# One decode step of attention with a gated unit: a kernel in a scheduling framework rewritten with hand-written waits, pairs of heads, three slots

## The chip, the cores and the metric

The kernel runs on one core of a Trainium2 chip. The core has TensorE (PE: matmuls, with PEld for loading their weights), VectorE (DVE), ScalarE (ACT), GpSimd (POOL) and SyncE (SP). SP and ACT issue transfers (DMA) between the chip's main memory and the on-chip memory, which has 128 partitions; 16 DMA engines carry them. The metric is the time of one execution in microseconds on the device, as the median of several runs.

## The reference

One token `x` of 512 numbers is normalised and goes through attention with 32 heads against caches of 8192 keys and values of 128 numbers, all in 32-bit floats, and through a gated unit. The two results are multiplied and added to `x`.

```python
xn = layernorm(x)                                   # (1, 1, 512)
q = (xn @ wq).reshape(32 heads, 128)                # wq: 512 x 4096
scores = einsum("hd,hkd->hk", q, k_cache) * 128 ** -0.5
o = einsum("hk,hkd->hd", softmax(scores), v_cache)  # caches: 32 x 8192 x 128
s = o.reshape(4096) @ wo                            # wo: 4096 x 512
h = sigmoid(xn @ w_gate) * (xn @ w_up)              # 512 x 1376 each
g = silu(h @ w_down)                                # w_down: 1376 x 512
out = x + s * g
```

K and V of one head are 4 MB each, 268 MB in all heads; `wq` and `wo` are 8 MB each, the three gate matrices 2.8 MB each.

## The kernel before

The kernel is written in a framework that places the waits, with the order of instructions written out by hand (`manual_schedule`). Each load goes into one of six slots of 32 KB a partition (`slot`, line 59). A head's K is one load of 4 MB in which each partition takes 64 keys, one row of 32 KB; V likewise. K and the weights are issued on SP's queue, V on ACT's (`load_rows`, line 96). `order` (line 110) is the order of loads: the two halves of wq, then K and V of each head, then the gate matrices and wo, in rows of 8 KB, between and behind the last heads; `need` issues ahead by it.

At the start, x is normalised (lines 155 to 167) and q is computed as matmuls with one column of weights, four of them side by side in four column groups of TensorE (line 182). `spread` copies the q of four heads to all partitions (line 192).

For each head, VectorE multiplies K by q and sums over the 128 numbers, in four blocks of 16 keys a partition (lines 258 and 259). It takes the maximum of each partition (line 263); TensorE turns these into a row (line 265) of which VectorE takes the maximum (line 269), but only after the first block of the next head. TensorE sends the maximum to all partitions (line 271), ScalarE takes the exponential and its sum (line 275), and TensorE multiplies it with V: 16 matmuls of 4 weight columns and 512 moving columns in four column groups (line 284). ScalarE copies the result and TensorE folds the four diagonal blocks (lines 288 and 290). Every fourth head, VectorE normalises four heads and turns them into columns (`heads_out`).

The gate's matmuls stand in the last head and behind it (`glu_row`, `glu_hidden`, `glu_out`), then `project` multiplies with wo, four groups of 128 columns for each row, and the result is written.

Of the kernel before, what the change touches and what calls it, by code (L numbers as in the profile page):

```python
# [17 lines left out]
@with_exitstack
def kernel(
# [35 lines left out]
    ps_o = ctx.enter_context(tc.tile_pool(name="ps_o", bufs=1, space=bass.MemoryType.PSUM))
    ps_s = ctx.enter_context(tc.tile_pool(name="ps_s", bufs=1, space=bass.MemoryType.PSUM))


    def slot(name):
        return stream.tile([P, SLOT], F32, tag="stream", name=name)  # L60

    xv = x.rearrange("a b d -> (a b d)")
    x_col = const.tile([P, KT], F32, name="x_col")
    x_row = const.tile([P, GC], F32, name="x_row")
    wq_t, kv_t, wo_t, gl = {}, {}, {}, {}

    def load_wq(i):
        n = KT // 2
        t = slot(f"wq{i}").rearrange("p (k c) -> p k c", k=n)
        nc.sync.dma_start(t, wq.rearrange("(p k) c -> p k c", k=KT)[:, i * n:(i + 1) * n, :])  # L70
        for k in range(n):
            wq_t[i * n + k] = t[:, k, :]

    def load_gate(name, src):
        t = slot(name)
        t = t[:, :KT * F].rearrange("p (k f) -> p k f", f=F)
        nc.sync.dma_start(t, src.rearrange("(p k) f -> p k f", k=KT))
        for k in range(KT):
            gl[name, k] = t[:, k, :]
# [4 lines left out]
    FW = FP * GP
    assert FW + GP <= QT and FL % GP == 0

    def load_down():
        t = slot("wd")
        n = (FP + 1) * D
        gl["hid"] = t[:, n:n + (FP + 1) * GP].rearrange("p (c i) -> p c i", i=GP)  # L90
        t = t[:, :n].rearrange("p (c e) -> p c e", e=D)
        nc.sync.dma_start(t[:, :FP, :], w_down[:FP * P, :].rearrange("(p r) e -> p r e", r=FP))
        nc.sync.dma_start(t[:FL, FP, :], w_down[FP * P:, :])
        gl["wd"] = t

    def load_rows(which, src, h):
        t = slot(f"{which}{h}")
        q = nc.sync if which == "k" else nc.scalar
        q.dma_start(t, src[0, h].rearrange("(p j) d -> p (j d)", p=P))
        kv_t[which, h] = t  # L100

    def load_wo(g0, n):
        t = slot(f"wo{g0}").rearrange("p (g r e) -> p g r e", r=HT, e=D)
        for i in range(n):
            src = wo[(g0 + i) * P * HT:(g0 + i + 1) * P * HT, :].rearrange("(p r) e -> p r e", r=HT)
            for r0, r1 in ((0, HT),) if g0 + i < NW - 1 else ((0, HT - 1), (HT - 1, HT)):
                nc.sync.dma_start(t[:, i, r0:r1, :], src[:, r0:r1, :])
            wo_t[g0 + i] = t[:, i]

    order = [("wq", 0), ("wq", 1)]  # L110
    for h in range(H):
        order.append(("k", h))
        if h < H - 2:
            order.append(("v", h))
    order += [("v", H - 2), ("glu", 0), ("v", H - 1), ("glu", 1), ("glu", 2), ("wo", 0), ("wo", NW // 2)]

    def issue(which, i):
        if which == "wq":
            load_wq(i)
        elif which == "wo":  # L120
            load_wo(i, NW // 2)
        elif which == "glu":
            (lambda: load_gate("wg", w_gate), lambda: load_gate("wu", w_up), load_down)[i]()
# [3 lines left out]
    ahead = iter(order)
    loaded = set()

    def need(*item):  # L130
        while item not in loaded:
            nxt = next(ahead)
            issue(*nxt)
            loaded.add(nxt)

    nc.scalar.dma_start(x_col, xv.rearrange("(p k) -> p k", k=KT))
    need("v", 1)
    nc.vector.memset(x_row, 0.0)
    nc.scalar.dma_start(x_row[0:P:GP, :], xv.rearrange("(g c) -> g c", g=NG))


    ones = const.tile([P, P], F32, name="ones")
    nc.vector.memset(ones, 1.0)
    ident = const.tile([P, P], F32, name="ident")
    make_identity(nc, ident)
    eps_t = const.tile([P, 1], F32, name="eps_t")
    nc.vector.memset(eps_t, EPS)

    def total(col, name):
        t = ps_s.tile([P, 1], F32, tag="ps_s", name=name)  # L150
        nc.tensor.matmul(t, ones, col, start=True, stop=True)
        return t

    st = const.tile([P, 8], F32, name="st")
    nc.vector.reduce_sum(st[:, 0:1], x_col, axis=AX.X)  # L155
    p_sum = total(st[:, 0:1], "p_sum")
    nc.vector.tensor_scalar(st[:, 1:2], p_sum, 1.0 / D, None, op0=ALU.mult)
# [6 lines left out]
    nc.scalar.activation(st[:, 3:4], p_sq, AF.Sqrt, bias=eps_t, scale=1.0 / D)
# [2 lines left out]
    nc.vector.tensor_scalar(xn, xc, st[:, 4:5], None, op0=ALU.mult)
# [8 lines left out]
    q_row = const.tile([P, NQ // NG, QT], F32, name="q_row")
    pq = [big(f"pq{b}", 0.0) for b in range(NQ // NG)]
    for k in range(KT):
        for b in range(NQ // NG):
            for g in range(NG):  # L180
                c = (b * NG + g) * QT
                nc.tensor.matmul(pq[b][g * GP:g * GP + 1, :], xn[:, k:k + 1], wq_t[k][:, c:c + QT],  # L182
                                 start=(k == 0), stop=(k == KT - 1))
    for b in range(NQ // NG):
        nc.scalar.copy(q_row[:, b, :], pq[b])

    qb = {}

    def spread(t):
        b, g = divmod(t, NG)  # L190
        pb = big(f"pb{t}")
        nc.tensor.matmul(pb, ones[g * GP:g * GP + 1, :], q_row[g * GP:g * GP + 1, b, :],  # L192
                         start=True, stop=True)
        qb[t] = work.tile([P, QT], F32, tag="qb", name=f"qb{t}")
        nc.scalar.copy(qb[t], pb)  # L195


    g_row = const.tile([P, GC], F32, name="g_row")
    pgu = {}

    def glu_row(name):

        pgu[name] = big(f"p{name}", 0.0)
        for c0, f0, w, m in ((0, 0, FW, NG), (FW, P * FP, GP, FL // GP)):
            for k in range(KT):
                for g in range(m):
                    nc.tensor.matmul(pgu[name][g * GP:g * GP + 1, c0:c0 + w], xn[:, k:k + 1],
                                     gl[name, k][:, f0 + g * w:f0 + (g + 1) * w],
                                     start=(k == 0), stop=(k == KT - 1))

    def glu_hidden():

        sg, h = q_row[:, 0, :FW + GP], q_row[:, 1, :FW + GP]
        nc.scalar.activation(sg, pgu["wg"][:, :FW + GP], AF.Sigmoid)
        nc.vector.tensor_mul(h, sg, pgu["wu"][:, :FW + GP])
        for t in range(FP):
            nc.vector.transpose(gl["hid"][:, t, :], h[:, t:FW:FP])
        nc.vector.transpose(gl["hid"][:, FP, :], h[:, FW:])

    def glu_out():  # L220
        pd = big("pd", 0.0)
        for t in range(FP + 1):
# [151 lines left out]
```

## Time and profile before

| | us |
|---|---|
| median of 3 runs | 695.82 (695.55 to 696.3) |
| span of the profiled execution, first to last instruction | 693.6 |
| VectorE busy | 606.3 |
| TensorE busy, matmuls | 296.0 |
| VectorE waiting for K | 37.6 |
| VectorE's first product with K starts at | 51.90 |

The profile gives the profiled execution's span; its own time with what lies around the span is not listed, so the span stands against the median of the runs. Busy times are totals for an engine, so an engine can be busy for most of the span and still not be the one that the end waits for. In a row of a group, the numbers are the busy time, the mean of one instruction in nanoseconds, and the idle time of the engine ahead of these instructions with what ended it. In a row of a timeline they are the start and the length in microseconds, the engine, the line and the instruction, and in brackets the idle time before.

### The profile page before, as it was taken

Reading aid. Unit: us, or ns where it says so; the run is one execution under the profiler, and the core shown is the slowest. Engines: PE = TensorE matmul, PEld = TensorE weight load, DVE = VectorE, ACT = ScalarE, POOL = GpSimd, SP = SyncE. Lnnn points to the kernel's source line nnn. Section 1 sums busy time; section 2 is a strip of 40 time slices with the busy share of each in tenths; the row PEclk is TensorE's granted clock in tenths of the full one; section 3 lists DMA queues with packets and bytes.
Section 4 is the critical chain, followed back from the end, with each engine's and each line's share of the span. In section 5 each row is a group of like instructions: output and inputs, shape, how many; then the busy total and the mean of one; then the engine's idle time right before and its main releaser. Section 6 shows DMA issues by size and latency. Waiting matters only on the chain.

```text
span 693.6 us, 4841 instructions
## 1 busy us (share of the span) xinstructions
PE 296.0 (43%) x2012; PEld 89.6 (13%) x2012; DVE 606.3 (87%) x418; ACT 49.0 (7%) x144; POOL 0.7 (0%) x6
## 2 busy tenths in 40 slices
PE   0420454434343554445434444445443434444555
PEld 0000110111110111111111111111110110111224
DVE  1109999999999999999999999999989999999931
ACT  0010110001000010000000100001000100000010
POOL 0000000000000000000000000000000000000000
PEclk9855676766666666666766666666666666666789
DMA  9999999999999999999999999999999999999996
GB/s 384 433 423 431 443 425 422 438 437 425 426 439 433 424 429 438 430 426 427 438 433 425 434 431 435 424 433 435 429 427 431 438 426 427 430 437 427 424 387 252
DMA packets 11526, 293.98 MB, mean 424 GB/s; under 512 B 1416, under 2 KB 1424, under 8 KB 1776
## 3 DMA queue, kind: packets, MB, share of 16 engines
q1 hardware_dynamic: 6744, 159.45, 53.9%
q10 hardware_dynamic: 4760, 134.22, 45.0%
q8 instruction: 15, 0.25, 0.1%
q14 instruction: 7, 0.06, 0.0%
HBM read 293.67 MB, written 0.00 MB: 423 GB/s over the span
## 4 chain that ended last, share of the span: by engine, by line
DVE 74%; DMA 20%; another core or an unknown queue 5%; issue 1%; PE 0%; DVEq 0%; SPq 0%; ACT 0%
DVE sc L259 36%; DVE k L258 34%; DMA k<-in_A_k_cache_dram 11%; DMA wd<-in_B_w_down_dram 4%; DMA wo<-in_A_wo_dram 3%; DMA x_col<-in_A_x_dram 2%; DVE mx L263 1%; DVE mx L269 1%; DVE ot L300 1%; DVE on L297 0%; DVE o_all L301 0%; PE acc L306 0%; DVE po L238 0%; DVE pq L173 0%
## 5 line engine op out<-in xcount | busy, mean ns | idle before, releaser
L258 DVE TENSOR_TENSOR k<-k,qb 128x2048 f32<-128x2048 f32 x128 | 291.8, 2280 | 37.6 <-DMA k<-in_A_k_cache_dram 37.6
L259 DVE TENSOR_REDUCE sc<-k 128x16 f32<-128x2048 f32 x128 | 292.6, 2286 | 6.5
L284 PE MATMUL po<-v,pr 128*4 128x512 f32 x1024 | 182.9, 877 | 0.0
L265 PE MATMUL pt<-ident,mx 128*1 128x128 f32 x64 | 18.3, 386 | 192.8 <-DVE mx L263 192.8
L271 PE MATMUL pm<-mx,ones 1*128 1x1 f32 x64 | 18.6, 358 | 122.6 <-DVE mx L269 122.6
L284 PEld LDWEIGHTS po<-v,pr 128*4 128x4 f32 x1024 | 33.3, 110 | 118.6 <-issue 118.6
L290 PE MATMUL pn<-o,pick 128*1 128x128 f32 x256 | 33.1, 272 | 22.8 <-ACT o L288 22.8
L271 PEld LDWEIGHTS pm<-mx,ones 1*128 1x128 f32 x64 | 15.9, 307 | 145.6 <-DVE mx L269 145.6
L288 ACT COPY o<-po 128x512 f32<-128x512 f32 x32 | 18.8, 586 | 187.2 <-PE po L284 187.2
L265 PEld LDWEIGHTS pt<-ident,mx 128*1 128x1 f32 x64 | 2.8, 80 | 202.5 <-DVE mx L263 171.1
L272 ACT ACTIVATE mx<-pm 128x1 f32<-128x1 f32 x32 | 5.5, 171 | 331.8 <-PE pm L271 331.8
L290 PEld LDWEIGHTS pn<-o,pick 128*1 128x1 f32 x256 | 18.8, 83 | 58.6 <-ACT o L288 53.8
L182 PE MATMUL pq<-wq,xn 128*1 128x512 f32 x64 | 12.0, 917 | 11.4 <-DMA wq<-in_A_wq_dram 10.0
L280 PE MATMUL pn<-ones,rs 128*1 128x1 f32 x64 | 6.0, 164 | 24.7 <-ACT pr L275 24.7
L192 PE MATMUL pb<-q_row,ones 1*128 1x512 f32 x16 | 15.6, 1074 | 0.0
L275 ACT ACTIVATE pr<-sc,mx 128x64 f32<-128x64 f32 x32 | 11.1, 348 | 1.0
L155 DVE TENSOR_REDUCE st<-x_col 128x1 f32<-128x4 f32 x1 | 0.2, 157 | 12.0 <-DMA x_col<-in_A_x_dram 12.0
L195 ACT COPY qb<-pb 128x512 f32<-128x512 f32 x8 | 4.7, 586 | 67.4 <-PE pb L192 67.4
L269 DVE TENSOR_REDUCE mx<-pt 1x1 f32<-1x128 f32 x32 | 8.6, 269 | 0.5 <-PE pt L265 0.5
L295 DVE RECIPROCAL rl<-pn 128x1 f32<-128x1 f32 x8 | 1.2, 148 | 8.7 <-PE pn L290 8.7
L306 PE MATMUL acc<-wo,o_all 128*1 128x128 f32 x256 | 7.7, 272 | 2.5 <-issue 1.5
L343 DVE TENSOR_TENSOR res<-g_row,acc 128x128 f32<-128x128 f32 x1 | 0.3, 286 | 9.5 <-PE acc L306 9.5
(56 smaller groups left out, 68.6 us busy)
## 6 DMA issues: line engine op xcount, KB each, us to landing
v<-in_A_v_cache_dram ACTq DMA_DIRECT2D x32, 4096.0 KB, 32.8
k<-in_A_k_cache_dram SPq DMA_DIRECT2D x32, 4096.0 KB, 34.9
wq<-in_A_wq_dram SPq DMA_DIRECT2D x2, 4096.0 KB, 31.2
wo<-in_A_wo_dram SPq DMA_DIRECT2D x7, 1024.0 KB, 22.0
wg<-in_B_w_gate_dram SPq DMA_DIRECT2D x1, 2752.0 KB, 38.1
wu<-in_B_w_up_dram SPq DMA_DIRECT2D x1, 2752.0 KB, 18.7
...
```

The source lines that it names most:

```text
L182: nc.tensor.matmul(pq[b][g * GP:g * GP + 1, :], xn[:, k:k + 1], wq_t[k][:, c:c + QT], start=(k == 0), stop=(k == KT - 1))
L192: nc.tensor.matmul(pb, ones[g * GP:g * GP + 1, :], q_row[g * GP:g * GP + 1, b, :], start=True, stop=True)
L258: nc.vector.tensor_mul(kt, kt, q)
L259: nc.vector.reduce_sum(sc[h][:, j:j + SB], kt, axis=AX.X)
L265: nc.tensor.matmul(pt, mx[h][:, 0:1], ident, start=True, stop=True)
L269: nc.vector.reduce_max(mx[h][:1, 1:2], pt, axis=AX.X)
L271: nc.tensor.matmul(pm, ones[:1, :], mx[h][:1, 1:2], start=True, stop=True)
L275: nc.scalar.activation(pr[h], sc[h], AF.Exp, bias=mx[h][:, 2:3], scale=SCALE, accum_out=rs[h])
L284: nc.tensor.matmul(po[h % 2][g * GP:g * GP + HT, :], pr[h][:, j:j + HT], kv_t["v", h][:, j * Dh:(j + HT) * Dh], start=(j < HT * NG), stop= ...
L288: nc.scalar.copy(o1, po[h % 2])
L290: nc.tensor.matmul(row[:, :Dh], pick[:, b:b + 1], o1[:, b * Dh:(b + 1) * Dh], start=(b == 0), stop=(b == HT - 1))
L306: nc.tensor.matmul(acc[g * GP:g * GP + 1, :], o_all[:, w, r:r + 1], wo_t[w][:, r, g * GC:(g + 1) * GC], start=(w + r == 0), stop=(w == NW ...
```

## The change

The kernel is written anew. All memory is placed by hand and every wait is written out on a semaphore (`Count`, `wait_ge`, `take`).

- Three slots A, B and C of 64 KB a partition take the place of six of 32 KB. K goes to B and A in turn, V always to C. All large loads are on SP's queue. One load holds K or V of two heads: 8 MB, 64 partitions for each head, one row of 64 KB a partition.
- The gate comes first: its matrices are loaded first, into A, then wq into C and the first half of K of pair 0 into B. The gate's intermediate results lie in the second half of B.
- q is made by matmuls with 64 equal weight columns, so that it comes out on all partitions at once: even heads on the upper 64, odd heads on the lower 64.
- VectorE's products and sums are in two blocks of 64 keys a partition, and the maximum of a pair follows directly, with VectorE waiting for TensorE's row.
- The exponentials of the two heads stand in two columns, each zero where the other head's partitions are (`prz`). One matmul has 8 weight columns, four blocks of keys for two heads, and 512 moving columns; 32 of them make a pair. TensorE's 15 first pairs are a hardware loop; V of the last pair goes to B.
- All heads are normalised and turned once at the end. wo comes in five pieces of 16, 8, 5, 2 and 1 rows of 2 KB a partition.

```diff
+    A, B, C = (over(f"slot{i}", SLOT, SLOTS + i * SLOT * 4) for i in range(3))
...
+    WO = ((0, 16), (16, 24), (24, 29), (29, 31), (31, 32))
...
+    k_src = k_cache[0].rearrange("h (p j) e -> (h p) (j e)", p=HALF)
+    v_src = v_cache[0].rearrange("h (p j) e -> (h p) (j e)", p=HALF)
+    k_slot = lambda n: (B, A)[n % 2]
...
+    d["wg"].by(sp.dma_start(wg_t, w_gate.rearrange("(p k) f -> p k f", k=KT)), 16)
+    d["x"].by(act.dma_start(x_col, xv.rearrange("(p k) -> p k", k=KT)), 16)
+    d["wu"].by(sp.dma_start(wu_t, w_up.rearrange("(p k) f -> p k f", k=KT)), 16)
+    d["wd"].by(sp.dma_start(wd_t, w_down[:FP * P, :].rearrange("(p r) e -> p r e", r=FP)), 16)
+    d["wd"].by(sp.dma_start(wd_rest[:FL, :], w_down[FP * P:, :]), 16)
+    d["wq"].by(sp.dma_start(wq_t, wq.rearrange("(p k) c -> p k c", k=KT)), 16)
+    d["ka"].by(sp.dma_start(B[:, :late], rows_of(k_src, 0, 0, late)), 16)
...
+    for name, t, banks in (("wg", wg_t, (4, 5, 6)), ("wu", wu_t, (0, 1, 2))):
+        pe.wait_ge(d[name].sem, 16)
+        for (f0, f1), b in zip(FC, banks):
+            for k in range(KT):
+                m = pe.matmul(bank[b][k * GP:k * GP + 1, :f1 - f0], xn[:, k:k + 1], t[:, k, f0:f1], start=True, stop=True)
...
+    for a, t in enumerate((g_sb, u_sb)):
+        for i in range(FP):
+            m = pe.matmul(turned[:, a, i:i + 1], t[:, i:FP * P:FP], sel, start=True, stop=True)
...
+    pe.wait_ge(d["wq"].sem, 16)
+    pe.wait_ge(s_dve.sem, n_xnb)
+    nt = NP // NG
+    for t in range(nt):
+        cols = wq_t[:, :, t * QT * 2:(t + 1) * QT * 2].rearrange("p k (i a d) -> p k a i d", a=2, d=Dh)
+        for k in range(KT):
+            for a in range(2):
+                m = pe.matmul(bank[3 + t][a * HALF:(a + 1) * HALF, :], xnb[:, k, :], cols[:, k, a],
+                              start=(k == 0), stop=(k == KT - 1))
+        n_q = s_pe.by(m)
+        act.wait_ge(s_pe.sem, n_q)
+        n_qc = s_act.by(act.copy(q_all[:, t * NG:(t + 1) * NG, :].rearrange("p n d -> p (n d)"), bank[3 + t]))
...
+    def scores(n, waits):
...
+            part = kt[:, i * h:(i + 1) * h, :]
+            s_dve.by(dve.tensor_mul(part, part, q))
+            self_wait()
+            s_dve.by(dve.reduce_sum(s[:, i * h:(i + 1) * h], part, axis=AX.X))
+        k_free[n] = s_dve.n
+        self_wait()
+        dve.reduce_max(mx[:, 0:1], s, axis=AX.X).then_inc(s_rm, 1)
+        dve.wait_ge(s_pt, n + 1)
+        dve.reduce_max(mx[:1, 2:4], pt[:1, :P].rearrange("p (a m) -> p a m", a=2), axis=AX.X).then_inc(s_am, 1)
...
+    def pair(v, waits):
+        take(pe, s_rm)
+        pe.matmul(pt[:1, :P], mx[:, 0:1], ident, start=True, stop=True).then_inc(s_pt, 1)
+        take(pe, s_am)
+        pe.matmul(pm[:, 0:2], ones[:1, :], mx[:1, 2:4], start=True, stop=True).then_inc(s_pm, 1)
+        take(pe, s_pr)
+        pe.matmul(oTl[:, 2:4], ones, rs2, start=True, stop=True)
+        nj = NB // ROWS
+        for j in range(nj):
+            if j in waits:
+                waits[j]()
+            g = j % NG
+            m = pe.matmul(po[g * GP:g * GP + 2 * ROWS, :], prz[:, j * ROWS:(j + 1) * ROWS, :],
+                          v[:, j * QT:(j + 1) * QT], start=(j < NG), stop=(j >= nj - NG))
+        m.then_inc(s_po, 1)
...
+    sp.wait_ge(s_pe.sem, n_gate)
+    d["k0"].by(sp.dma_start(B[:, late:], rows_of(k_src, 0, late, SLOT)), 16)
+    load_k(1)
+    dve.wait_ge(s_act.sem, n_qc)
...
+    sp.wait_ge(s_pe.sem, n_q)
+    for n in range(NP - 1):
+        if n:
+            sp.wait_ge(s_po, n)
+        sp.dma_start(C, rows_of(v_src, n)).then_inc(d_v, 16)
+        if n + 2 < NP:
+            sp.wait_ge(s_dve.sem, k_free[n])
+            load_k(n + 2, 2 if n + 2 == NP - 1 else 1)
+    sp.wait_ge(s_dve.sem, k_free[NP - 2])
+    d["va"].by(sp.dma_start(B[:, :late], rows_of(v_src, NP - 1, 0, late)), 16)
+    d["vb"].by(sp.dma_start(B[:, late:], rows_of(v_src, NP - 1, late, SLOT)), 16)
+    sp.wait_ge(s_po, NP - 1)
+    for (r0, r1), c in zip(WO, d_wo):
+        c.by(sp.dma_start(wo_t[:, r0:r1, :], wo.rearrange("(p r) e -> p r e", r=RW)[:, r0:r1, :]), 16)
+
+    with nc.Fori(0, NP - 1, engines=[pe.engine], head_slot={pe.engine: 0}):
+        pair(C, {0: lambda: take(pe, d_v, 16)})
+    pair(B, {0: lambda: pe.wait_ge(d["va"].sem, 16), NB // ROWS // 2: lambda: pe.wait_ge(d["vb"].sem, 16)})
```

More of the change, by code (lines that the diff above doesn't have):

```diff
@@ L55 @@
[L55 to L79, printed above, removed]
     FP = F // P
     FL = F - FP * P
[L84 to L123, printed above, removed]
-        else:
-            load_rows(which, k_cache if which == "k" else v_cache, i)
@@ L127 @@
[L127 to L157, printed above, removed]
@@ L184 @@
[L184 to L222, printed above, removed]
-            m = P if t < FP else FL
-            for g in range(NG):
-                nc.tensor.matmul(pd[g * GP:g * GP + 1, :GC], gl["hid"][:m, t, 0:1],
-                                 gl["wd"][:m, t, g * GC:(g + 1) * GC],
-                                 start=(t == 0), stop=(t == FP))
-        nc.scalar.activation(g_row, pd[:, :GC], AF.Sigmoid)
-        return pd
@@ L331 @@
-    need(*order[-1])
-    all_max(H - 1, pt)
-    values(H - 1)
-    glu_row("wu")
-    heads_out(NW - 1)
-    glu_hidden()
-    pd = glu_out()
-    nc.vector.tensor_mul(g_row, g_row, pd[:, :GC])
-    for w in range(NW):
-        project(w)
-    res = const.tile([P, GC], F32, name="res")
-    nc.vector.tensor_mul(res, g_row, acc)
-    nc.vector.tensor_add(res, res, x_row)
-    nc.sync.dma_start(out.rearrange("a b (g c) -> (a b g) c", g=NG), res[0:P:GP, :])
+    QT = 512
+    RW = H * Dh // P
+    SLOT = NB * Dh
@@ new lines @@
+    wd_rest = put("o1", QT)
+    o1 = wd_rest
+    sc = [put("sc0", NB), put("sc1", NB)]
+    ident = put("ident", P)
+    ones = put("ones", P)
+    prz = put("prz", NB * 2).rearrange("p (j a) -> p j a", a=2)
+    x_row = put("x_row", GC)
+    g_row = put("g_row", GC)
+    heads = put("heads", NP * 4).rearrange("p (n c) -> p n c", c=4)
+    o_norm = put("o_norm", H)
+    o_turn = put("o_turn", H)
+    o_all = put("o_all", RW)
+    pick = put("pick", ROWS * 2)
+    sel = pick[:, 0:1]
+    mx = put("mx", 8)
@@ new lines @@
+    wd_t = A[:, 2 * KT * F:2 * KT * F + FP * D].rearrange("p (r e) -> p r e", e=D)
+    wq_t = C.rearrange("p (k c) -> p k c", k=KT)
+    wo_t = C.rearrange("p (r e) -> p r e", e=D)
+    late = SLOT // 2
+    g_sb = B[:, late:late + F]
+    u_sb = B[:, late + F:late + 2 * F]
+    d_sb = B[:, late + 2 * F:late + 2 * F + D]
+    bank = [nc.alloc_psum_tensor(f"bank{i}", [P, QT], F32).ap() for i in range(8)]
+    po, pt, pm, acc, fold_ps, o_ps, oTl = bank[0], bank[1], bank[2], bank[4], bank[5], bank[6], bank[7]
@@ new lines, with self_wait, total @@
+    dve.memset(prz.rearrange("p j a -> p (j a)"), 0.0)
+    for b in (0, 1, 2, 4, 5, 6):
+        dve.memset(bank[b], 0.0)
+    dve.memset(bank[7][:, :2 * (FP + 1)], 0.0)
+    dve.wait_ge(s_pool.sem, 2)
+    for g in range(NG):
+        n_set = s_dve.by(dve.tensor_copy(pick[g * GP:(g + 1) * GP, :], ident[g * GP:(g + 1) * GP, g * GP:g * GP + ROWS * 2]))
+    def self_wait():
+        dve.wait_ge(s_dve.sem, s_dve.n)
+    def total(col, at):
+        pe.wait_ge(s_dve.sem, s_dve.n)
+        n = s_pe.by(pe.matmul(bank[3][:, at:at + 1], ones, col, start=True, stop=True))
+        return n
@@ new lines @@
+    dve.wait_ge(s_act.sem, n)
+    n = s_dve.by(dve.tensor_mul(hid, sg, turned[:, 1, :]))
+    pe.wait_ge(s_dve.sem, n)
+    pe.wait_ge(d["wd"].sem, 32)
+    for t in range(FP + 1):
+        c, m = t % NG, P if t < FP else FL
+        w = wd_t[:, t, :] if t < FP else wd_rest[:FL, :]
+        m = pe.matmul(bank[0][c * GP:c * GP + 1, :], hid[:m, t:t + 1], w, start=(t < NG), stop=(t + NG > FP))
+    n = s_pe.by(m)
+    act.wait_ge(s_pe.sem, n)
+    n = s_act.by(act.copy(d_sb, bank[0]))
+    pe.wait_ge(s_act.sem, n)
@@ new lines @@
+    for g in range(NG):
+        m = pe.matmul(bank[1][g * GP:g * GP + 1, :GC], sel, d_sb[:, g * GC:(g + 1) * GC], start=True, stop=True)
+    n_gate = s_pe.by(m)
+    act.wait_ge(s_pe.sem, n_gate)
+    n = s_act.by(act.activation(g_row, bank[1][:, :GC], AF.Sigmoid))
+    dve.wait_ge(s_act.sem, n)
+    n_grow = s_dve.by(dve.tensor_mul(g_row, g_row, bank[1][:, :GC]))
+    pe.wait_ge(d["wq"].sem, 16)
[10 more added lines that the diff above has]
+        n_qc = s_act.by(act.copy(q_all[:, t * NG:(t + 1) * NG, :].rearrange("p n d -> p (n d)"), bank[3 + t]))
@@ new lines, in softmax @@
+    def softmax(n):
+        act.wait_ge(s_pm, n + 1)
+        s_act.by(act.mul(mx[:, 4:6], pm[:, 0:2], -SCALE))
+        act.wait_ge(s_act.sem, s_act.n)
+        for a in range(2):
+            r = slice(a * HALF, (a + 1) * HALF)
+            e = act.activation(prz[r, :, a], sc[n % 2][r, :], AF.Exp, bias=mx[r, 4 + a:5 + a], scale=SCALE,
+                               accum_out=rs2[r, a:a + 1])
+        e.then_inc(s_pr, 1)
+        act.wait_ge(s_po, n + 1)
+        act.copy(o1, po).then_inc(s_o1, 1)
+        act.wait_ge(s_ot, n + 1)
+        s_act.by(act.copy(heads[:, n, :], oTl[:, 0:4]))
@@ new lines, in pair @@
+    def pair(v, waits):
[13 more added lines that the diff above has]
+        m.then_inc(s_po, 1)
+        take(pe, s_o1)
+        for b in range(ROWS):
+            m = pe.matmul(oTl[:, 0:2], o1[:, b * Dh:(b + 1) * Dh], pick[:, 2 * b:2 * b + 2],
+                          start=(b == 0), stop=(b == ROWS - 1))
+        m.then_inc(s_ot, 1)
@@ new lines @@
+    dve.wait_ge(s_act.sem, s_act.n)
+    hn = heads[:, :, 2:4]
+    s_dve.by(dve.reciprocal(hn, hn))
+    self_wait()
+    s_dve.by(dve.tensor_mul(o_norm.rearrange("p (n a) -> p n a", a=2), heads[:, :, 0:2], hn))
+    self_wait()
+    n = s_dve.by(dve.transpose(o_turn, o_norm))
+    pe.wait_ge(s_dve.sem, n)
+    n = s_pe.by(pe.matmul(o_ps[:, :RW], turn, o_turn, start=True, stop=True))
+    dve.wait_ge(s_pe.sem, n)
+    n = s_dve.by(dve.tensor_copy(o_all, o_ps[:, :RW]))
+    pe.wait_ge(s_dve.sem, n)
@@ new lines @@
+    FOLD = WO[1][1]
+    for (r0, r1), c in zip(WO, d_wo):
+        pe.wait_ge(c.sem, 16)
+        for r in range(r0, r1):
+            if r < FOLD:
+                g = r % NG
+                m = pe.matmul(fold_ps[g * GP:g * GP + 1, :], o_all[:, r:r + 1], wo_t[:, r, :],
+                              start=(r < NG), stop=(r >= FOLD - NG))
+            else:
+                for g in range(NG):
+                    m = pe.matmul(acc[g * GP:g * GP + 1, :GC], o_all[:, r:r + 1],
+                                  wo_t[:, r, g * GC:(g + 1) * GC], start=(r == FOLD), stop=(r == RW - 1))
+        if r1 == FOLD:
+            n = s_pe.by(m)
+            act.wait_ge(s_pe.sem, n)
+            n_f = s_act.by(act.copy(o1, fold_ps))
+        if r1 == WO[2][1]:
+            pe.wait_ge(s_act.sem, n_f)
+            for g in range(NG):
+                pe.matmul(acc[g * GP:g * GP + 1, :GC], sel, o1[:, g * GC:(g + 1) * GC], start=False, stop=False)
@@ L349 @@
+    n = s_pe.by(m)
+    dve.wait_ge(d["xr"].sem, 16)
+    dve.wait_ge(s_pe.sem, n)
+    s_dve.by(dve.tensor_mul(res, g_row, acc[:, :GC]))
+    self_wait()
+    n = s_dve.by(dve.tensor_add(res, res, x_row))
+    sp.wait_ge(s_dve.sem, n)
+    d["out"].by(sp.dma_start(out.rearrange("a b (g c) -> (a b g) c", g=NG), res[0:P:GP, :]), 16)
+    sp.wait_ge(d["out"].sem, 16)
 _INS = ['A_x', 'A_k_cache', 'A_v_cache', 'A_wq', 'A_wo', 'B_w_gate', 'B_w_up', 'B_w_down']
```

242 lines of the change are left out of this document (120 added, 122 removed).

## The prediction

> **What bounds the kernel now.** I read the page first: shares, the DMA slices, then the queues and the groups of VectorE.
>
> ```profile
> span 693.6 us, 4841 instructions
> PE 296.0 (43%) x2012; PEld 89.6 (13%) x2012; DVE 606.3 (87%) x418; ACT 49.0 (7%) x144; POOL 0.7 (0%) x6
> DMA  9999999999999999999999999999999999999996
> q1 hardware_dynamic: 6744, 159.45, 53.9%
> q10 hardware_dynamic: 4760, 134.22, 45.0%
> HBM read 293.67 MB, written 0.00 MB: 423 GB/s over the span
> L259 DVE TENSOR_REDUCE sc<-k 128x16 f32<-128x2048 f32 x128 | 292.6, 2286 | 6.5
> L258 DVE TENSOR_TENSOR k<-k,qb 128x2048 f32<-128x2048 f32 x128 | 291.8, 2280 | 37.6 <-DMA k<-in_A_k_cache_dram 37.6
> ```
>
> VectorE has 87% of the span and the chain that ended last is mostly VectorE, but the 16 DMA engines are full in 39 of 40 slices, with two queues sharing them, and VectorE's only long wait (37.6 us) is for K. So the bound is the transfer of 293.67 MB; VectorE is a close second. Stretches of the span, chosen by the size of the rows moved, give the price of a byte (columns: length, the busy time of PE, PEld, DVE, ACT, POOL, clock, DMA share, GB/s):
>
> ```profile
> 0.00:10.00 10.00, 0.00 (x0) 0.00 (x0) 0.31 (x3) 1.28 (x1) 0.70 (x6) 1.00 0.89 354
> 100.00:640.00 540.00, 236.81 (x1324) 65.89 (x1312) 528.11 (x332) 37.63 (x119) 0.00 (x0) 0.68 1.00 431
> 645.00:656.00 11.00, 6.68 (x50) 2.19 (x54) 10.72 (x8) 1.20 (x4) 0.00 (x0) 0.66 1.01 432
> 664.00:669.00 5.00, 4.67 (x26) 0.98 (x30) 0.00 (x0) 0.28 (x2) 0.00 (x0) 0.50 0.95 309
> 669.00:681.00 12.00, 8.22 (x208) 5.72 (x204) 3.94 (x21) 2.61 (x4) 0.00 (x0) 0.98 1.01 416
> 688.00:693.60 5.60, 1.26 (x40) 0.63 (x32) 0.58 (x2) 0.00 (x0) 0.00 (x0) 0.98 0.03 12
> ```
>
> 100 to 640 us is K and V in rows of 32 KB, 645 to 656 mostly gate weights in rows of 22 KB, 669 to 681 wo in rows of 8 KB; the last two stretches are from SP's queue alone. DMA begins near 1.1 us (share 0.89 of ten) and ends near 689: 4.6 us of the span are its tail.
>
> The sum is made against the profiled span, 693.6 us; the median of 695.82 lies 2.2 us above it, for what lies around the span, and I carry that 2.2 over. A difference under 0.2% (1.4 us) counts as no change.
>
> **The change, part by part.**
>
> *Larger pieces.* One round (a row on each of 16 engines) takes 16 x 32,768 B / 431 GB/s = 1.216 us, at 8 KB 131,072 B / 416 GB/s = 0.315 us. If each row has a fixed part, it is (4 x 0.315 - 1.216) / 3 = 0.015 us. K, V and wq make 33 transfers of 8.39 MB, 264 rounds of 64 KB rows (2.418 us each, 19.35 us a transfer) in place of 528: 264 x 0.015 = 3.9 us saved. But 22 KB rows already reach 432, so the fixed part may not be seen above 22 KB, or a 64 KB row may be cut in two: then 0. I take 3.0, nearer the end that the 8 KB row gives, since its size difference is the larger. wo in rows of 32, 16, 10, 4 and 2 KB in place of 8 and fewer: about 1.0 less (8.39 MB at 416 is 20.2, at 431 19.5; small rows remain at the end). Fewer unrolled PE instructions to fetch: 0.3.
>
> *VectorE, per pair.*
>
> ```profile
> 328.26 2.29 DVE L259 TENSOR_REDUCE sc<-k 128x16 f32<-128x2048 f32 x1
> 330.46 2.28 DVE L258 TENSOR_TENSOR k<-k,qb 128x2048 f32<-128x2048 f32 x1
> 332.78 2.29 DVE L259 TENSOR_REDUCE sc<-k 128x16 f32<-128x2048 f32 x1
> 335.10 0.22 DVE L263 TENSOR_REDUCE mx<-sc 128x1 f32<-128x64 f32 x1
> 335.38 0.58 PE L265 MATMUL pt<-ident,mx 128*1 128x128 f32 x2 [4.53 <-DVE mx L263]
> 339.83 0.27 DVE L269 TENSOR_REDUCE mx<-pt 1x1 f32<-1x128 f32 x1
> ```
>
> A product and a sum over 2048 elements take 332.78 - 328.26 = 4.52 us, 2.32 where the next depends, 2.20 where not. L263 reads 64 elements in 0.22, so (2.29 - 0.22) / 1984 = 1.04 ns an element: 8192 elements stream in 8.55, plus 0.1 to 0.2. A pair's four long instructions: 4 x 8.69 = 34.8 us, against 36.2 before (8 x 4.52). The maximum now stands on VectorE's path: 0.3, then PE's 0.58 with 0.1 of signals, then 0.27: about 1.2, which the next head's products covered before. Pair: 36.0 us. A pair's K and V take 38.7 us by DMA, so VectorE keeps up, with 2.7 spare; it saves nothing at the end, since DMA is the bound.
>
> *One slot for V, three in all.* V of the next pair waits on SP for PE's last value matmul, and behind it on SP waits the next K.
>
> ```profile
> 341.49 5.44 PE L284 MATMUL po<-v,pr 128*4 128x512 f32 x30
> 360.10 6.36 PE L284 MATMUL po<-v,pr 128*4 128x512 f32 x29
> 360.86 0.17 PEld L284 LDWEIGHTS po<-v,pr 128*4 128x4 f32 x4 [0.69 <-issue]
> 361.72 0.17 PEld L284 LDWEIGHTS po<-v,pr 128*4 128x4 f32 x4 [0.69 <-issue]
> ```
>
> Four column groups run side by side; a pass of four takes 0.85 at the half clock (361.72 - 360.86), two passes a matmul. A head is 16 matmuls, a pair of heads in one matmul 32: the same columns, 8 steps of 1.71, at most 13.7 us. The previous K occupies the DMA for 19.35 us after V's end; 13.7 plus about 1.2 for landing and 1.1 for the next start (0.89 share above) leaves 3.3. Hidden. So costs 0; without that cover each microsecond costs 14. The loop's jump and the four folding matmuls come after that signal, while PE waits for V.
>
> *One queue.* The 645 and 669 rows show SP's queue alone, through several transfers, at share 1.01. So 0. The Trainium skill (DMA: Bandwidth & Descriptors, Anatomy of one DMA) gives each DMA 2.0 us plus its bytes at 436 GB/s; paid one after another, 33 x 21.2 = 701 us would replace 642, 59 us more. Those shares near 1 speak against that where the next transfer is queued early.
>
> *Gate first.* It adds no bytes; its PE work moves from the end to the start, under wq's transfer. The issue of K0's second half and K1 now waits on SP for the gate, V0 for q, K2 for scores of pair 0.
>
> ```profile
> 13.13 0.16 DVE L155 TENSOR_REDUCE st<-x_col 128x1 f32<-128x4 f32 x1 [11.99 <-DMA x_col<-in_A_x_dram]
> 13.34 0.50 PEld L151 LDWEIGHTS p_sum<-st,ones 128*128 128x128 f32 x2 [13.34 <-DVE st L155]
> 15.95 0.23 DVE L167 TENSOR_SCALAR xn<-xc,st 128x4 f32<-128x4 f32 x1
> 20.19 0.15 PEld L182 LDWEIGHTS pq<-wq,xn 128*1 128x1 f32 x4 [0.71 <-issue]
> 21.00 0.10 PEld L182 LDWEIGHTS pq<-wq,xn 128*1 128x1 f32 x4 [0.66 <-issue]
> 21.43 0.09 PEld L182 LDWEIGHTS pq<-wq,xn 128*1 128x1 f32 x4 [0.34 <-issue]
> L164 ACT ACT_TABLE_LOAD x1 | 1.3, 1283 | 3.3 <-issue 3.3
> L288 ACT COPY o<-po 128x512 f32<-128x512 f32 x32 | 18.8, 586 | 187.2 <-PE po L284 187.2
> 51.90 2.29 DVE L258 TENSOR_TENSOR k<-k,qb 128x2048 f32<-128x2048 f32 x1 [31.97 <-DMA k<-in_A_k_cache_dram]
> ```
>
> All at the half clock: x behind eight 22 KB rows in place of 32 KB ones, 9.9 us; 3.05 to xn, as 13.13 to 16.18, plus a table load of 1.3: 14.2. Gate and up, 3 steps of 1.71 each: 24.5. Copies 1.8: 26.3. 22 turns with 128-column weights, 0.50 each: 37.3. Sigmoid with table load and product, 2.0; down, 3 steps, 5.1; copy and fold, 1.6: 46 us. By bytes at 431 GB/s after the first ten microseconds, plus 1.4 for a slow end of w_down like the 309 row, wq ends at 42.3 and K0's first half at 52.0. K0's second half must be issued by 50.9: in time, stall 0, cover 5 us.
>
> q: 32 matmuls with 64 output columns, two side by side, 16 steps. The warm pass is 0.43 (21.43 - 21.00), and the longest slow burst above lasted 6.4. With 6.8 us at 1.71 a step and twelve steps at 0.85 it takes 17, from about 44.5: 61.5, VectorE starts at 62.3 with the copy (51.9 before). K0's second half, K1 and V0 end on DMA at 61.7, 81.1 and 100.4. K2 needs pair 0's last sum at 62.3 + 34.8 = 97.1 and 1.1 to start: 98.2. Stall 0, with 2 us of cover.
>
> *The end.* The gate's tail goes; DMA ends last anyway.
>
> ```profile
> 689.05 1.05 PE L306 MATMUL acc<-wo,o_all 128*1 128x128 f32 x32 [0.85 <-DMA wo<-in_A_wo_dram]
> 690.17 0.29 DVE L343 TENSOR_TENSOR res<-g_row,acc 128x128 f32<-128x128 f32 x1 [9.47 <-PE acc L306]
> 690.81 0.66 SPq L345 DMA_DIRECT2D out_dram<-res  x1
> ```
>
> After the last wo piece 4 matmuls remain in place of 16 (their records are double): 1.05 becomes about 0.5. The last V pair (two halves of 6.8 us at the slow clock, then some 4 of folds and turns) ends while wo's 19.5 us run. Saved 0.5.
>
> Sum: 3.0 + 1.0 + 0.3 + 0.5 = 4.8 us off, nothing added: span 688.8, with 2.2 around it 691.0.
>
> **Rivals.**
> - *The pieces gain nothing* (cut in two, or no fixed part above 22 KB, as 432 at 22 KB suggests): 691.0 + 3.0 = 694.0, about the edge of no change.
> - *q comes late, the load stops at K2* (the slower side). VectorE starts 10 us later than before already. If PE stays at the half clock through q (16 x 1.71 = 27.3, from 46.3) or 64-column halves do not overlap (32 x 0.85), VectorE starts at 74.3, K2 is issued at 109.1 and the DMA stands 9.8 us: 700.8. It decides from a stall of 6.2 us, VectorE starting after 70.7. For it: the slow bursts of 6.4 us; against: 21.00 to 21.43, the clock rises in a burst.
> - *V's single slot is late each pair*: past 17.0 us of value matmuls, 14 us for each microsecond; at 18.0 it is 705. Against: 13.7 at the slow clock.
> - *Gaps between transfers of one queue*: by the skill's 2.0 us each, 59 us, hence 750. Against: share 1.01 on SP alone.
>
> **How the numbers follow.** Main case 0.50 (its own range 687 to 694.3: below, the pieces at 3.9, the 1.4 of the 309 row and the 0.7 that the first ten microseconds lack gone, with 1 us for rounding of the 431; above, 3.3 us of small stalls), pieces gain nothing 0.14, late q 0.18 (half of its cases below the price), V's slot 0.07, gaps 0.03, things not thought of 0.08, mostly slower. Predicted: 691.0. Faster by over 0.2% (below 694.4): 0.49 of the main case, 0.08 of the second, 0.04 of the third, 0.01 of the rest: 0.62. Same (to 697.2): 0.06 + 0.05 + 0.02 = 0.13. Slower: 0.25. The range holds the main case, the second and the late q to its price: 686.5 to 701.
>
> **What would show it.** DMA share near 1.00 from 2 us to the end and about 433 GB/s in the middle: the pieces. A dent near 50 us: the gate was late; near 100 us: q was late; dents every 39 us: V's slot or gaps. VectorE's first product near 62 us, and its long instructions near 8.65 us each, with waits for K of some 2 us a pair. The forecast is wrong if any dent adds to more than 5 us, or if GB/s in the middle stays at 431 or falls.

## The result: 1.05% faster, and the profile after

| | before | after |
|---|---|---|
| median of 4 runs, us | 695.68 (695.5 to 696.3) | 688.39 (688.09 to 689.1) |
| span of the profiled execution, us | 693.6 | 686.7 |

The ratio is 0.9895 (95% interval 0.9881 to 0.9909): 7.3 us less, where 4.8 were forecast. A second measurement of the changed kernel beside the first experiments gave 688.62 and the same ratio; experiments are compared with that.

Lines of the page of the changed kernel, answering to those shown of before:

```profile
span 686.7 us, 3607 instructions
PE 241.3 (35%) x1560; PEld 84.6 (12%) x1560; DVE 572.5 (83%) x132; ACT 39.9 (6%) x127; POOL 0.7 (0%) x6
DMA  8999999999999999999999999999999999999996
q1 hardware_dynamic: 6456, 293.67, 98.9%
HBM read 293.67 MB, written 0.00 MB: 428 GB/s over the span
L279 DVE TENSOR_TENSOR slot<-slot,q_all 128x8192 f32<-128x8192 f32 x32 | 277.8, 8682 | 41.6 <-ACT q_all L260 23.2
L281 DVE TENSOR_REDUCE sc<-slot 128x64 f32<-128x8192 f32 x32 | 277.9, 8686 | 1.1
```

The bytes are the same, one queue carries them, and the slices show no dent: the transfers are still the bound, and they ended earlier because each byte cost less. VectorE lost 33.8 us of work (606.3 to 572.5). The same stretch of both kernels, 120 to 560 us (columns as in the prediction), first before, then after:

```profile
120.00:560.00 440.00, 195.33 (x1086) 54.45 (x1078) 431.33 (x274) 31.65 (x99) 0.00 (x0) 0.68 1.00 431
```
```profile
120.00:560.00 440.00, 131.54 (x864) 44.59 (x864) 413.60 (x72) 22.08 (x82) 0.00 (x0) 0.61 1.00 434
```

431 against 434 GB/s at share 1.00 is most of the gain. The start and the steady state of the changed kernel, in its timeline:

```profile
38.01 0.33 SPq L326 DMA_DIRECT2D slot<-in_A_k_cache_dram  x1
44.21 16.93 PE L256 MATMUL bank<-slot,xnb 128*64 128x512 f32 x64 [6.26 <-DMA slot<-in_A_wq_dram]
61.81 8.69 DVE L279 TENSOR_TENSOR slot<-slot,q_all 128x8192 f32<-128x8192 f32 x1 [23.19 <-ACT q_all L260]
96.56 0.33 SPq L267 DMA_DIRECT2D slot<-in_A_k_cache_dram  x1
97.84 8.67 DVE L279 TENSOR_TENSOR slot<-slot,q_all 128x8192 f32<-128x8192 f32 x1
102.30 8.27 PE L316 MATMUL bank<-slot,prz 128*8 128x512 f32 x48 [0.48 <-PEq L129]
...
334.07 8.46 PE L316 MATMUL bank<-slot,prz 128*8 128x512 f32 x64 [17.49 <-PEq L129]
342.60 0.33 SPq L341 DMA_DIRECT2D slot<-in_A_v_cache_dram  x1
```

The numbers in brackets are the forecast's. The gate is done at 38.0 (46 at worst, needed by 50.9), q takes 16.9 us (17), VectorE starts at 61.8 (62.3), a pair takes it 97.84 - 61.81 = 36.0 us (36.0), and the third K is issued at 96.6 (97.1) while V of the first pair lands near 101. Each V is issued as its predecessor's 8.5 us of matmuls end. The end, from the chain that ended last:

```profile
671.67 0.22 DVE o_turn L365
...
672.85 8.01 PE bank L379 x48
680.86 1.09 PE bank L383 x40
681.95 0.22 PE bank L392 x8
682.17 0.71 PE bank L383 x24
```

TensorE works on wo almost without a pause from 672.9 to 682.9, and the chain leads from there to the heads, not to a transfer. The last row of wo lands at 681.6, so the heads' chain and wo's transfers end nearly level.

### The profile page after: what moved, and what is told of

The parts are those of the page before. It is cut to its first block, busy times and chain, and to the rows that moved or that the text cites. A ratio compares the mean times of both kernels' runs of the same rounds, so it can differ in the third digit from the quotient of the medians.

```text
span 686.7 us, 3607 instructions
## 1 busy us (share of the span) xinstructions
PE 241.3 (35%) x1560; PEld 84.6 (12%) x1560; DVE 572.5 (83%) x132; ACT 39.9 (6%) x127; POOL 0.7 (0%) x6
## 5 line engine op out<-in xcount | busy, mean ns | idle before, releaser
L279 DVE TENSOR_TENSOR slot<-slot,q_all 128x8192 f32<-128x8192 f32 x32 | 277.8, 8682 | 41.6 <-ACT q_all L260 23.2
L281 DVE TENSOR_REDUCE sc<-slot 128x64 f32<-128x8192 f32 x32 | 277.9, 8686 | 1.1
L316 PE MATMUL bank<-slot,prz 128*8 128x512 f32 x1024 | 147.2, 739 | 220.5 <-PEq L129 220.5
L316 PEld LDWEIGHTS bank<-slot,prz 128*8 128x8 f32 x1024 | 30.2, 103 | 324.0 <-issue 324.0
L299 ACT COPY o<-bank 128x512 f32<-128x512 f32 x16 | 9.4, 586 | 380.0 <-PE bank L316 380.0
L321 PE MATMUL bank<-pick,o 128*128 128x2 f32 x128 | 16.4, 250 | 12.8 <-PEq L129 12.8
L256 PE MATMUL bank<-slot,xnb 128*64 128x512 f32 x64 | 16.9, 695 | 6.3 <-DMA slot<-in_A_wq_dram 6.3
L321 PEld LDWEIGHTS bank<-pick,o 128*128 128x128 f32 x128 | 15.5, 191 | 27.2 <-issue 27.2
L295 ACT ACTIVATE prz<-sc,mx 64x128 f32<-64x128 f32 x32 | 13.0, 406 | 0.7
L223 PE MATMUL bank<-pick,slot 128*128 128x1 f32 x40 | 9.3, 365 | 1.8 <-DVE slot L216 1.8
```

Of the source, the lines that this page charges most:

```text
L223: m = pe.matmul(turned[:, a, i:i + 1], t[:, i:FP * P:FP], sel, start=True, stop=True)
L256: m = pe.matmul(bank[3 + t][a * HALF:(a + 1) * HALF, :], xnb[:, k, :], cols[:, k, a], start=(k == 0), stop=(k == KT - 1))
L279: s_dve.by(dve.tensor_mul(part, part, q))
L281: s_dve.by(dve.reduce_sum(s[:, i * h:(i + 1) * h], part, axis=AX.X))
L295: e = act.activation(prz[r, :, a], sc[n % 2][r, :], AF.Exp, bias=mx[r, 4 + a:5 + a], scale=SCALE, accum_out=rs2[r, a:a + 1])
L299: act.copy(o1, po).then_inc(s_o1, 1)
```

## The experiments

**1. Row size: 32 KB rows on the same queue.** Every 64 KB load becomes two of 32 KB rows; waits count twice as much.

```diff
-        w = SLOT // parts
-        for i in range(parts):
-            c = k_sem(n) if i == parts - 1 else d["ka"]
+        w = SLOT // 2
+        for i in range(2):
+            c = k_sem(n) if parts == 1 or i == parts - 1 else d["ka"]
...
```

> Every 64 KB row is cut into two transfers of 32 KB rows, same queue, same slots, same waits. Theory of the row size (the prediction's: a fixed part of 0.015 us a row, 264 rounds more): 3.0 to 3.9 us slower than the changed kernel, 691.4 to 692.3. Rival, theory of the single queue (what the transfers gained comes from V no longer sharing the engines with K from a second queue, and the row size adds only what the profile's rates leave): at most 2.2 us slower, 688.4 to 690.6, with the rate of the middle staying near 433 GB/s. Rival, no gain from transfers at all (the gain is VectorE's or the moved gate's): 688.4 unchanged.

Measured: 689.90 (689.59 to 690.0), ratio 0.9914 (0.99 to 0.9927): 1.3 us slower than the changed kernel, whose runs beside it ended between 688.4 and 688.94. The row size is real, and about 0.4 of what was forecast.

```profile
120.00:560.00 440.00, 132.59 (x864) 44.76 (x864) 411.60 (x72) 22.07 (x82) 0.00 (x0) 0.60 1.00 433
```

With the old row size the middle still moves 433 GB/s, not 431. In the trace's transfer records a 64 KB row takes 2419.4 ns on average in the changed kernel, a 32 KB row 1213.8 here, but 1219.9 before. For each round (a row on each of the 16 engines) the size is worth 2 x 1213.8 - 2419.4 = 8.2 ns. The changed kernel has 240 rounds of 64 KB, so this is 2.0 us; the first K, the last K and the last V are loaded in halves of 32 KB rows. Rows of the same size being faster, 6.1 ns over 528 rounds of 32 KB, is worth 3.2 us.

**2. One queue in the kernel before.** V goes on SP's queue; nothing else.

```diff
-        q = nc.sync if which == "k" else nc.scalar
+        q = nc.sync
```

> The kernel before, with one edit: V is issued on SP's queue too, so all large loads share one queue. Rows stay 32 KB, six slots. Theory of the single queue: 3.0 to 3.5 us faster than the kernel before, ratio 0.995, and a rate in the middle near 433 GB/s in place of 431. Theory of the row size: no change, ratio 1.000. If V behind K's wait on the same queue lets the transfers run dry, slower, and the DMA shares show dents.

Measured: 695.97, ratio 1.0009 (1.0001 to 1.0018). The theory of the single queue falls: 32 KB rows still take 1219.9 ns.

```profile
120.00:560.00 440.00, 191.14 (x1056) 52.91 (x1048) 422.27 (x268) 30.43 (x95) 0.00 (x0) 0.68 1.00 431
```

The records of the kernel before show when its rows lengthen: 318 of the 323 rows between 13.5 and 37.8 us take exactly 1213 ns, while TensorE works on q. Then one DMA engine after another goes over to rows of 1214 to 1224 ns, and nearly all later rows stay there. Of the 70 rows that begin between 45 and 50 us, 58 already take that long, though since 40 us no engine but ScalarE has worked, and that one only until 40.5:

```profile
40.00:50.00 10.00, 0.00 (x0) 0.00 (x0) 0.00 (x0) 0.46 (x1) 0.00 (x0) 0.57 1.04 449
```

So reads of TensorE or VectorE beside the transfers are not what keeps the rows long.

The Trainium skill (DMA: Bandwidth & Descriptors, Issuing engines are not separate DMA queues) says that transfers from several engines run on the same 16 DMA engines and interleave. By that rule one queue or two is the same bandwidth; this run agrees, 431 and 431.

**3. Two queues in the changed kernel.** V is issued by ScalarE, after its wait for the last value matmul.

```diff
         act.wait_ge(s_po, n + 1)
+        if n + 1 < NP - 1:
+            act.dma_start(C, rows_of(v_src, n + 1)).then_inc(d_v, 16)
         act.copy(o1, po).then_inc(s_o1, 1)
...
+    act.dma_start(C, rows_of(v_src, 0)).then_inc(d_v, 16)
...
-        if n:
-            sp.wait_ge(s_po, n)
-        sp.dma_start(C, rows_of(v_src, n)).then_inc(d_v, 16)
```

> V is issued on ACT's queue, right after the wait for the last value matmul that ScalarE has anyway; K stays on SP's. Rows stay 64 KB. Theory of the row size: the middle keeps its rate, and only the order of landing changes: 688.4, within 1 us. Theory of the single queue: rows of two queues taking turns cost what they cost before (528 rounds of 32 KB lost about 3 to 3.5 us), so 1.7 to 3.5 us slower, 690.1 to 691.9, and a rate in the middle below 433 GB/s. K landing later beside V may add a few us of waits of VectorE, in either theory, if the transfers ever run dry.

Measured: 748.28 (746.5 to 752.7), 60 us slower, by far outside both expectations. The middle stretch, and two issues in it:

```profile
120.00:560.00 440.00, 119.54 (x786) 39.86 (x786) 376.99 (x66) 20.16 (x75) 0.00 (x0) 0.60 0.92 394
```
```profile
369.13 40.17 SPq L267 DMA_DIRECT2D slot<-in_A_k_cache_dram  x2
371.55 0.33 ACTq L300 DMA_DIRECT2D slot<-in_A_v_cache_dram  x1
410.61 9.24 PE L318 MATMUL bank<-slot,prz 128*8 128x512 f32 x64 [33.66 <-PEq L129]
```

The first row holds two issues of K, one at 369 and one near 409. K and V are issued at 369 and 372, share the engines, and V is there only when both are, 39 us later. Meanwhile no slot is free for a further load, and the transfers run dry (share 0.92). On one queue the first of the two lands after 19 us. By experiment 2 the queue was worth nothing as bandwidth; here its order costs 60 us, with three slots where the kernel before had six.

**4. The distance of rows in memory.** As experiment 1, but each half is one whole head on 128 partitions, so that neighbouring partitions read 32 KB apart, as before.

```diff
-        return src[n * P:(n + 1) * P, lo:hi]
+        cache = k_cache if src is k_src else v_cache
+        return cache[0, 2 * n + (lo > 0)].rearrange("(p j) e -> p (j e)", p=P)
...
```

> The changed kernel with 32 KB rows on one queue, as in the run of 689.9 us, but each 4 MB half of a load is now one whole head on 128 partitions: the rows that neighbouring partitions read lie 32 KB apart in memory, as in the kernel before, in place of 64 KB. Everything else, waits and lengths included, is the same; q stays as it was, so half of the scores are those of another head's q. Open is why K and V rows of 32 KB took 1219.9 ns in the kernel before, with one queue as with two, and 1213.8 in that run: 3.2 us of the gain. Theory of the pitch: 1218 to 1220 ns and 3 us slower, 692.5 to 693.5. Rival, the cause lies in the kernel before (its slots, its bursts of TensorE and ScalarE): 1213 to 1214 ns and 689.9, within 0.7.

Measured: 689.48 (689.35 to 690.25), rows 1213.9 ns. The distance is not what made rows slow in the kernel before.

**5. VectorE in eight blocks,** as long as before.

```diff
-        h = NB // 2
+        h = NB // 8
...
-        for i in range(2):
+        for i in range(8):
...
```

> The changed kernel with VectorE's products and sums in eight blocks of 16 keys a partition, as long as before (2048 elements), in place of two. VectorE needs 8 x 4.52 + 1.2 = 37.4 us a pair in place of 36.0, against 38.7 of transfers. Theory that the transfers are the bound: 688.4, within 1 us; pair 0's scores end 1.4 us later, inside the cover of 3 us that the trace shows at the third K. Rival, VectorE sets the time and the larger blocks made the gain: 16 x 1.4 = 22 us slower, 711.

Measured: 692.84 (691.46 to 694.72), 4.2 us slower: neither 0 nor 22. Rows take 2419.7 ns, so the block length is not what made rows slow either. The end of its timeline:

```profile
659.57 0.29 DVE L284 TENSOR_REDUCE mx<-sc 128x1 f32<-128x128 f32 x1
676.98 8.01 PE L379 MATMUL bank<-slot,o_all 128*1 128x512 f32 x48 [0.28 <-DVE o_all L369]
```

In the changed kernel these stand at 655.84 and 672.85. In the middle the longer pair hides under the transfers (434 GB/s at share 1.00 from 120 to 560 us, as in the changed kernel), but pairs 14 and 15 follow each other without a wait for K, and the heads' chain, which in the changed kernel ends nearly level with wo's transfers, moves by 4.1 us with the end behind it.

**6. The gate first, alone, in the kernel before.** Its loads lead the order, its matmuls stand before q, wo is loaded behind the last V.

```diff
-    order = [("wq", 0), ("wq", 1)]
+    order = [("glu", 0), ("glu", 1), ("glu", 2), ("wq", 0), ("wq", 1)]
...
+    glu_row("wg")
+    glu_row("wu")
+    glu_hidden()
+    pd = glu_out()
+    nc.vector.tensor_mul(g_row, g_row, pd[:, :GC])
...
```

> The kernel before with the gate moved to the start (its three matrices loaded first, its matmuls before q), and wo behind the last V; nothing else changes. Theory: 8.5 MB of loads and the gate's steps stand before the first K, so VectorE starts some 20 us later, near 72, and at 37.8 us a pair (605 us in all) ends near 677 with the last values, the heads and 20 us of project and output behind it: VectorE becomes the bound, 3 to 10 us slower than the kernel before. So the gate's place alone would lose, and is paid for by the shorter pair. Rival, the moved gate itself makes the gain (its work leaves the end): 3 to 7 us faster.

Measured: 701.28 (700.65 to 701.88), ratio 1.0076 (1.0062 to 1.0091): 5.8 us slower.

```profile
L265 DVE TENSOR_TENSOR k<-k,qb 128x2048 f32<-128x2048 f32 x128 | 292.0, 2282 | 39.9 <-DMA k<-in_A_k_cache_dram 39.9
56.29 2.29 DVE L265 TENSOR_TENSOR k<-k,qb 128x2048 f32<-128x2048 f32 x1 [22.46 <-DMA k<-in_A_k_cache_dram]
660.70 2.29 DVE L265 TENSOR_TENSOR k<-k,qb 128x2048 f32<-128x2048 f32 x1 [0.52 <-DMA k<-in_A_k_cache_dram]
679.16 0.22 DVE L270 TENSOR_REDUCE mx<-sc 128x1 f32<-128x64 f32 x1
696.73 0.29 DVE L344 TENSOR_TENSOR res<-g_row,acc 128x128 f32<-128x128 f32 x1 [5.59 <-PE acc L313]
```

The size came as expected, but not the mechanism. VectorE starts at 56.3, only 4.4 us later than before and not 20, and waits for K 25 times in place of 8: it is not the bound. With the gate's bytes in front, K arrives later throughout; the first product with the last head's K stands at 660.7, where it stood at 643.0 before. VectorE ends its scores at 679 in place of 662, and values, heads and project follow. The last load ends at 688.7, about as before (689.2), but 11.4 us of work stand behind it in place of 4.4. So with the gate's loads at the end, transfers go on while that work is done; with these loads at the start they are over sooner than the work. Whether the shorter pair pays for the gate's place in the changed kernel was not tested.

**7. q twice,** to move VectorE's start by a known amount.

```diff
-        for k in range(KT):
+        for k in (*range(KT), *range(KT)):
```

> The matmuls of q are done twice over, in the same banks; the sum is then twice q, so the scores are those of 2q. Price: 16 more steps of 0.86 us at the full clock, 13.7 us, so VectorE starts at 75.5 in place of 61.8. In the trace the third K is issued at 96.6 and the transfers reach it at 100.9, with 1.1 to start: 3.2 us of cover. The prediction's rival of the late q: a dent of 13.7 - 3.2 = 10.5 us there, and 10.5 us slower, 699. Rival, the loss is caught up later because VectorE's pair is shorter than the transfers': less than 3 us slower.

Measured: 700.81, 12.2 us slower; VectorE starts at 75.6, as expected. The stretch 95 to 113 us, in the changed kernel and here:

```profile
95.00:113.00 18.00, 11.68 (x70) 3.13 (x70) 17.16 (x5) 3.02 (x7) 0.00 (x0) 0.63 1.06 459
```
```profile
95.00:113.00 18.00, 1.14 (x4) 0.61 (x4) 17.16 (x5) 0.56 (x2) 0.00 (x0) 0.50 0.43 175
```

The dent is 57% of 18 us, 10.3 us, where the cover of 3.2 us (the time by which the third K was early in the changed kernel) gave 10.5. It is not caught up, so the prediction's rival of the late q is a real mechanism, 3 us away. The other 1.9 us of the 12.2 were not traced to a cause.

**8. and 9. Value matmuls twice and three times,** the extra ones into a bank that nobody reads.

```diff
-        for j in range(nj):
+        for j in range(nj * (extra + 1)):
...
+            if j < nj * extra:
+                pe.matmul(bank[3][g * GP:g * GP + 2 * ROWS, :], prz[:, j % nj * ROWS:(j % nj + 1) * ROWS, :],
+                          v[:, j % nj * QT:(j % nj + 1) * QT], start=True, stop=True)
+                continue
+            j -= nj * extra
...
```

> In each pair of the loop the 32 value matmuls are first done into a bank that nobody reads, then as they were: a burst of 8.5 us becomes 15.3. V of the next pair is issued 10.8 us before the K ahead of it has landed, 1.1 of which it needs to start: cover 9.7. So no change, 688.4 within 1 us. The prediction's threshold of 17.0 us says the same. Rival, V's single slot is already tight: slower by more than 5 us.

> The same with two extra sets: a burst of about 22.2 us, past the threshold of 17.0 us by 5.2 and past the trace's cover by 4.0. Expected 14 x 4.0 to 14 x 5.2 = 56 to 73 us slower, 744 to 761, with a dent in the DMA share in each pair. If the burst were hidden by something else, 688.4.

Measured: twice, 698.15 as the median of eight runs spread from 694.2 to 701.6; three times, 778.27. The traced run of the first is the fastest of its eight, 5.6 us slower than the changed kernel. Two stretches of it, and one pair:

```profile
110.00:300.00 190.00, 86.12 (x662) 26.68 (x654) 182.13 (x32) 9.51 (x35) 0.00 (x0) 0.69 0.99 423
300.00:600.00 300.00, 143.51 (x1136) 42.33 (x1136) 272.18 (x48) 15.20 (x56) 0.00 (x0) 0.72 1.00 433
118.45 0.33 SPq L346 DMA_DIRECT2D slot<-in_A_v_cache_dram  x1
277.87 0.33 SPq L346 DMA_DIRECT2D slot<-in_A_v_cache_dram  x1
```
```profile
300.13 9.01 PE L317 MATMUL bank<-slot,prz 128*8 128x512 f32 x64 [17.23 <-PEq L129]
308.95 7.04 PE L321 MATMUL bank<-slot,prz 128*8 128x512 f32 x64
315.47 0.29 DVE L284 TENSOR_REDUCE mx<-sc 128x1 f32<-128x128 f32 x1
316.06 0.33 SPq L346 DMA_DIRECT2D slot<-in_A_v_cache_dram  x1
318.17 0.28 DVE L286 TENSOR_REDUCE mx<-bank 1x2 f32<-1x128 f32 x1 [2.41 <-PE bank L306]
319.37 8.69 DVE L279 TENSOR_TENSOR slot<-slot,q_all 128x8192 f32<-128x8192 f32 x1 [0.92 <-DMA slot<-in_A_k_cache_dram]
```

Bursts below the threshold of 17.0 already lose: the first five, of 15.3 to 16.5 us, end so late that the next V is issued late. The second pair's V is issued at 118.4; by the transfer records the first of the 16 engines is ready for its next row at 119.4 and the last at 121.7. The next three V are issued 0.3 to 1.6 us ahead of the first engine, and the one at 277.9 comes 0.4 us behind it. The first rows of these five transfers take 2.67 to 3.11 us on average in place of 2.42. By 300 us the transfers are 5.6 us behind those of the changed kernel and by 589 us 6.1: hardly more is lost. In the pair shown, with a burst of 15.9 us, V is issued 2.1 us ahead, and although VectorE waits 2.4 us there for its maximum, whose matmul stands behind the burst on TensorE, the transfers lose nothing. Why other runs lose up to 13 us is not shown, as they have no trace.

With three times, 89.7 us are lost, more than the 56 to 73 expected. In 15 stretches of 4.4 to 5.8 us all 16 engines stand idle, and by the sums of the records the engines are idle for 79 us more than in the changed kernel. The records make the other 10: the first row of each engine behind such a stretch takes 3.0 to 3.2 us, nearly all others 2.42.

**10. The loop written out.**

```diff
-    with nc.Fori(0, NP - 1, engines=[pe.engine], head_slot={pe.engine: 0}):
+    for _ in range(NP - 1):
```

> The changed kernel with TensorE's 15 pairs written out in place of the loop. Theory: some eleven blocks of 16 KB of instructions more are fetched, at one row's time on one engine each: 11 x 1.1 / 16 = 0.8 us slower at most, 688.4 to 689.2. Rival, the loop's jump costs time each pair on the path: faster, below 687.5. Rival, the loop is what keeps fetches out of the transfers' way: over 1 us slower.

Measured: 689.97 (689.66 to 690.93), ratio 0.992 (0.9907 to 0.9933), about 1.4 us slower; the intervals touch, so the size is uncertain. By the sums of the transfer records it is 0.8. Its queue of instructions, and that of the changed kernel:

```profile
q8 instruction: 12, 0.20, 0.1%
```
```profile
q8 instruction: 4, 0.07, 0.0%
```

**11. wo in 8 KB rows.**

```diff
-        c.by(sp.dma_start(wo_t[:, r0:r1, :], wo.rearrange("(p r) e -> p r e", r=RW)[:, r0:r1, :]), 16)
+        for q0 in range(r0, r1, 4):
+            q1 = min(q0 + 4, r1)
+            c.by(sp.dma_start(wo_t[:, q0:q1, :], wo.rearrange("(p r) e -> p r e", r=RW)[:, q0:q1, :]), 16)
...
```

> Only wo changes: its pieces of 16, 8 and 5 rows are cut into transfers of at most 4 rows, 8 KB a partition, as in the kernel before; the waits of the pieces stay. By the prediction's term for wo 1.0 us slower, 689.4; by the slower end in the trace of before up to 1.5. If the end is not set by the transfer of wo but by the matmuls behind it: 688.4.

Measured: 688.25 (688.14 to 688.66): no difference, though the records of the transfers are 0.5 us longer in sum. The two sides are nearly level at the end: here TensorE waited for pieces, and its matmuls with the first 24 rows took 7.0 us in place of 8.0, which hides the difference.

```profile
672.50 7.03 PE L381 MATMUL bank<-slot,o_all 128*1 128x512 f32 x48 [0.60 <-DMA slot<-in_A_wo_dram]
680.41 1.27 PE L385 MATMUL bank<-slot,o_all 128*1 128x128 f32 x40 [0.89 <-DMA slot<-in_A_wo_dram]
```

## Why the prediction was right, and where its terms were off

The mechanism held: the transfers are the bound before and after, the new waits hide, and what changes is the cost of a byte. By the sums of the transfer records, a sixteenth of all engines' time each, the 16 engines were busy for 687.5 us before and 679.8 after: 7.7 less. K, V and wq make 5.2 of it (644.1 to 638.9), wo 1.4 and instructions 0.8; the rest is small. The span's gain of 6.9 is this, less about 0.7 that the end got longer: behind the last load stand 5.1 us in place of 4.4. That the sum of 4.8 came as near as it did is partly luck, since its largest term was too large and a larger one was left out. The terms:

- *Larger pieces, 3.0.* Too large: experiment 1 measured 1.3, the records 2.0. The rounds of 64 KB are 240 and not 264, and the fixed part is 8.2 ns and not 15. The 15, 0.015 us, came from 8 KB rows at the end of the kernel before, and those were slow for another reason as well: they took 329 ns there and 309.6 in experiment 11.
- *Left out: rows of the same size got faster, 3.2.* This is the largest single piece of the gain, and the prediction has no term for it. It is not the queue (experiment 2), not the pitch (4), not VectorE's block length (5). In the kernel before the rows lengthen near 40 us, and stay long while neither TensorE nor VectorE works (experiment 2). What lengthens them stays open.
- *wo, 1.0.* The records of its transfers saved 1.4, but the end does not show it (experiment 11).
- *The end, 0.5 saved.* It was lost instead: after the last transfer stand TensorE's matmuls with wo, which start only when the last pair's heads are done at 672.8. The prediction let the last pair end while wo is loaded, and counted on the matmuls keeping up; the pair's scores end 36 us behind those of pair 14, and by 672.8 about 4.9 of wo's 8 MB have landed and wait.
- *VectorE, saves nothing at the end.* Wrong by 4.2 (experiment 5): the shorter pair is what keeps the heads' chain level with the transfers at the end.
- *The loop, 0.3.* The prediction gave no working for it. Between the two kernels the records of instruction transfers fell by 0.8, and experiment 10 gave 0.8 by records and about 1.4 by time, with the uncertainty said there.
- *The start, no stall, cover of 2 us.* Right: 3 us of cover, and experiment 7 shows the price behind it.
- *V's single slot.* Right that it hides: the burst took 8.5 us where 13.7 at the slow clock was allowed for. Wrong in its threshold of 17.0. The 16 engines do not end a load together: in the first pairs of experiment 8 the first is ready for its next row 2.3 us before the last, and the value matmuls start behind the last. So V's issue came too late with bursts of 15.3 us already.
- *One queue, no gaps.* Right, 1.00 throughout. Of the two rows taken as proof, the one at 645 was not SP's queue alone: by the transfer records the last V, on ACT's queue, landed at 651.4. Experiment 2 is the proof. The 2.0 us that the rival took from the Trainium skill (DMA: Bandwidth & Descriptors, Anatomy of one DMA) are given there for transfers that GpSimd issues. On SP's queue the first rows of a load queued in time took 2.42 us here, like all others.
